# A mixer and an MLP on one core: pair 8 ahead of pair 6, tile 0's transpose copied in halves, tile 3 transposed by DMA

## The chip, the core and the metric

The kernel runs on one core of a Trainium2 chip. The core has five engines with instruction queues of their own: TensorE (PE in the profile; its weight loads are PEld), VectorE (DVE), ScalarE (ACT), GpSimd (POOL) and SyncE (SP), which here only issues DMAs. They meet through semaphores. The metric is the device time of one execution in microseconds, the median over several runs.

## What is computed

```python
B, S, D, F = 1, 2048, 512, 1792
def reference(x, w1, w2, w3, w4):
    h = _gelu(_layernorm(x, axis=-1) @ w1)
    c = D // 4          # four groups of 128 columns, shifted by +1, -1, +2, -2 rows of S
    g0 = jnp.pad(h[:, :, 0*c:1*c], ((0, 0), (1, 0), (0, 0)))[:, :S, :]
    g1 = jnp.pad(h[:, :, 1*c:2*c], ((0, 0), (0, 1), (0, 0)))[:, 1:, :]
    g2 = jnp.pad(h[:, :, 2*c:3*c], ((0, 0), (2, 0), (0, 0)))[:, :S, :]
    g3 = jnp.pad(h[:, :, 3*c:   ], ((0, 0), (0, 2), (0, 0)))[:, 2:, :]
    hs = jnp.concatenate([g0, g1, g2, g3], axis=-1) @ w2
    x1 = x + hs
    h2 = _gelu(_layernorm(x1, axis=-1) @ w3) @ w4
    return x1 + h2
```

All inputs and the output are bf16.

## The kernel before

The 2048 rows are 16 tiles of 128 rows, held with rows on the partitions. A matmul needs its operand with columns on the partitions, so each tile has to be transposed before each of the two layer norms' products: either by TensorE (four transposes of 128x128 into PSUM, then a copy to SBUF by ScalarE), or by a DMA that transposes on its way.

The first product (x normalised, times w1) is done in two ways.

- **Tiles 0 to 5, "raw"**: x itself is transposed and multiplied by w1 (`m1r`), and the norm is applied afterwards, with the column sums of w1 (`cs0`, `cs1`, `cs2`, `cs`: matmuls of ones with w1's four parts). Tiles 0 to 3 are transposed by TensorE (`tp0` to `tp3`, copied by `ev0` to `ev3`), tiles 4 and 5 by one DMA straight from DRAM (`tdx_4`). `rc` copies the raw product out of PSUM.
- **Tiles 6 to 15, in pairs**: VectorE takes statistics (`st0_`, `ag0_`), GpSimd the inverse roots (`rs0_`), VectorE normalises (`nm0_`), and then the pair is transposed, by TensorE for pairs 8 and 10 (`tp8`, `ev8`), by DMA for the others (`td0_6`). `m1p` multiplies a pair in 16 matmuls of 256 columns, `g1p` or `g1s` applies the gelu.

The second product (`m2`, with w2 and shifted windows), the second norm, `m3`/`m3h` (w3) and `m4` (w4) follow. The first half pair of `m3h` needs `td1_8`, the second `td1_10`, both DMA transposes of the normalised second layer.

Each step is an `Op` of a small program, with the resources that it reads and writes. `emit` derives the semaphore waits from these. The order on each engine is written out by hand, in `firsts`: one list of names for PE, ACT, DVE, POOL and SP. An engine runs its list strictly in order, so a step that waits holds up everything after it on its engine. On SP, where nearly all loads and all transposing DMAs are issued, the list is the DMA queue's order. PSUM has eight banks; the number given to a step (`b`) says which ones it writes, and whoever wrote or read them last must be done.

At the start the lists before are (cut):

```python
firsts["pe"] = """wu tp0 cs0 cs1 m1r01 m1r02 tp1 m1r03 cs2 m1r0 cs tp2 m1r12 m1r1 tp3 m1r2 m1r3 m1r4 m1r5 tp8 m1p6
    tp10 m1p8 m1p10 ...
firsts["act"] = """ldw10 ldw12 ldx1 table ev0 ev1 rc0 ev2 ev3 rc1 rc2 rc3 rc4 rc5 ev8 cse g1p6 ev10 g1p8 g1s10 ...
firsts["sp"] = """ldx0 ldw11 ldx6 ldw13 ldx7 ldx2 ldx8 ldx3 ldx9 tdx_4 ldx10 ldx11 ldx12 td0_6 ldx13 ...
```

`wu` is seven matmuls of ones, issued before the first data is there. `m1r01` is tile 0's product with w1's first part alone, `m1r02` with the second, and so on, so that each can start when its part has landed.

Of the kernel before, what the change touches and what calls it, by code (L numbers as in the profile page):

```python
# [5 lines left out]
P = 128  # L6
ACT_F = mybir.ActivationFunctionType
# [19 lines left out]
class Program:  # L27
# [7 lines left out]
    def add(self, eng, name, fn, reads=(), writes=(), dma=False):  # L35
        self.ops.append(Op(name, eng, fn, reads, writes, dma))
# [135 lines left out]
def bass_standalone__mixer_s_mlp__prompt_kernel(nc: bass.Bass, x, w1, w2, w3, w4, out):  # L172
# [4 lines left out]
    DC = D // P  # L177
# [5 lines left out]
    xd = x[0].rearrange("(p t) d -> p t d", t=NT)  # L183
# [4 lines left out]
    with ExitStack() as es:  # L188
        sb = lambda name, shape, dt: es.enter_context(nc.sbuf_tensor(name, shape, dt))
        x_sb = sb("x_sb", [P, NT, D], BF16)  # L190
# [3 lines left out]
        xnT = sb("xnT", [P, NT, DC, P], BF16)  # L194
# [11 lines left out]
        ident = sb("ident", [P, P], BF16)  # L206
# [3 lines left out]
        neghalf = sb("neghalf", [P, 4], F32)  # L210
# [3 lines left out]
        psb = ps[:, :].bitcast(BF16)  # L214
# [27 lines left out]
        W1 = [(("w1", c), 0) for c in range(DC)]  # L242
        W2 = [(("w2", c), 0) for c in range(DC)]
        pr = Program()
        add = pr.add

        def bank(b, n=1):
            return ps[:, 512 * b : 512 * (b + n)]

        def bres(b, n, tag):  # L250
            return [(("ps", b + i), tag) for i in range(n)]
# [19 lines left out]
        def load_x(t, n, eng="sp"):  # L271
            add(eng, f"ldx{t}", lambda e: e.dma_start(x_sb[:, t : t + n, :], xd[:, t : t + n, :]),
                writes=[(("x", i), 0) for i in range(t, t + n)], dma=True)
# [9 lines left out]
        def dst_of(layer, t):  # L283
            return (xn, t, ("xn", t), 0) if layer == 0 else (x1n, POS[t] % 8, ("x1n", POS[t] % 8), t)
# [50 lines left out]
            add(eng, f"ev{t}", f, reads=bres(b, 1, f"tp{t}"), writes=[(("xT", i), 0) for i in range(t, t + n)])  # L335


        def tdma(layer, t, n):
            dst = xnT if layer == 0 else x1nT
            src, k = dst_of(layer, t)[:2]  # L340
            p0 = t if layer == 0 else POS[t]
            add("sp", f"td{layer}_{t}",
                lambda e: e.dma_start(dst[:, p0 : p0 + n, :, :].rearrange("p t c s -> p (t c) s"),
                                      src[:, k : k + n, :].rearrange("p t d -> p (t d)"), transpose=True),
                reads=[dst_of(layer, i)[2:] for i in range(t, t + n)],
                writes=[(("xT", i) if layer == 0 else ("x1T", i), 0) for i in range(t, t + n)], dma=True)


        def tdma_x(t):
            add("sp", f"tdx_{t}",  # L350
                lambda e: e.dma_start(xnT[:, t : t + 2, :, :].rearrange("p t c s -> p (t c) s"),
                                      xd[:, t : t + 2, :].rearrange("p t d -> p (t d)"), transpose=True),
                writes=[(("xT", i), 0) for i in (t, t + 1)], dma=True)

        def tdma_h(t, n):
            add("sp", f"th_{t}",
# [17 lines left out]
        def m1r(t, b, c0=0, c1=DC):  # L374
            def f(e):
                ins = None
                for c in range(c0, c1):
                    ins = e.matmul(bank(b), xnT[:, t, c, :], w1_sb[:, c, :], start=(c == 0), stop=(c == DC - 1))  # L378
                return ins

            rd = [(("xT", t), 0)] + W1[c0:c1]
            if c0:
                rd += bres(b, 1, f"m1r{t}{c0}")
            end = f"{c1}" if c1 < DC else ""
            add("pe", f"m1r{t}{end}", f, reads=rd, writes=bres(b, 1, f"m1r{t}{end}"))

        def rc(t, b):
            add("act", f"rc{t}", lambda e: e.activation(yraw[:, t, :], bank(b), ACT_F.Copy),
                reads=bres(b, 1, f"m1r{t}"), writes=[(("yraw", t), 0)])
# [11 lines left out]
                reads=[(("zraw", t % 4), t), (("rstd", t), 0)], writes=[(("hraw", t), 0)])  # L401


        def m1p(t, b):
            def f(e):
                ins = None
                for fc in range(DC):
                    dst = ps[:, 512 * b + 256 * fc : 512 * b + 256 * (fc + 1)]
                    for c in range(DC):
                        ins = e.matmul(dst, w1_sb[:, c, P * fc : P * (fc + 1)], xnT[:, t : t + 2, c, :],  # L410
                                       start=(c == 0), stop=(c == DC - 1))
                return ins

            add("pe", f"m1p{t}", f, reads=[*W1, (("xT", t), 0), (("xT", t + 1), 0)],
                writes=bres(b, 2, f"m1p{t}"))

        def g1p(t, b):
            src = bank(b, 2).rearrange("p (j t s) -> p j t s", j=DC, t=2)
# [139 lines left out]
        load_w1(2, "act")  # L558
        load_w1(3, "sp")
        load_x(1, 1, "act")  # L560
        for t, n in ((6, 1), (7, 1), (2, 1), (8, 1), (3, 1), (9, 1), (10, 1), (11, 1), (12, 1), (13, 1), (14, 1), (15, 1), (4, 2)):
            load_x(t, n)
        for c in range(DC):
            load_w2(c)
# [7 lines left out]
            colsum(4, c)  # L572
        colsum_out(4)
        for t in range(R):
            if t < 4:
                tp(t, 1, 6 + t % 2, True)
                ev(t, 1, 6 + t % 2, "act")
            elif t == 4:
                tdma_x(t)
            cuts = [0, 1, 2, 3, 4] if t == 0 else [0, 2, 4] if t == 1 else [0, 4]  # L580
            for c0, c1 in zip(cuts, cuts[1:]):
                m1r(t, YB[t], c0, c1)
            rc(t, YB[t])
# [7 lines left out]
        for t in range(R, NT, 2):  # L591
# [2 lines left out]
                ev(t, 2, 6 + t // 2 % 2)  # L594
            else:
                tdma(0, t, 2)
        for t, b in ((6, 2), (8, 4), (10, 0), (12, 2), (14, 6)):
            m1p(t, b)
            if t == 10:
                g1s(t, b, 0)  # L600
                g1s(t, b, 1)
            else:
                g1p(t, b)
# [19 lines left out]
        for t in (8, 10):  # L623
# [7 lines left out]
            tdma(1, t, 2)  # L631

        firsts = {}
        firsts["pe"] = """wu tp0 cs0 cs1 m1r01 m1r02 tp1 m1r03 cs2 m1r0 cs tp2 m1r12 m1r1 tp3 m1r2 m1r3 m1r4 m1r5 tp8 m1p6
            tp10 m1p8 m1p10 m2_8a m2_9a m2_8 m2_9b m2_9 m2_10a m2_11a m2_12a m2_13a m1p12 m1p14 m2_10 m2_11
            m2_12b m2_13b m2_14a m2_15a m2_12 m2_13 m2_14b m2_15b m2_14 m2_15""".split()
        firsts["act"] = """ldw10 ldw12 ldx1 table ev0 ev1 rc0 ev2 ev3 rc1 rc2 rc3 rc4 rc5 ev8 cse g1p6 ev10 g1p8 g1s10 g1s11
            g1r0 g1r1 g1p12 g1p14 g2h_0_0_0 g2h_0_0_4 g1r2 g1r3 g2h_0_0_8 g2h_0_0_12 g1r4 g1r5""".split()
        firsts["dve"] = """pada padb padc padd pade padf st0_0 st0_6 st0_7 ag0_6 ag0_7
            st0_8 nm0_6 nm0_7 st0_9 ag0_8 ag0_9 st0_10 st0_11 nm0_8 nm0_9 ag0_10 ag0_11  # L640
            st0_12 nm0_10 nm0_11 st0_13 ag0_12 ag0_13 st0_14 st0_15 ag0_14 ag0_15 nm0_12 nm0_13 st0_1 ag0_0 ag0_1
            nm0_14 nm0_15 zr0 zr1 x1_8 x1_9 st1_8 st1_9 ag1_8 ag1_9 st0_2 nm1_8 nm1_9 st0_3 ag0_2 ag0_3 x1_10 x1_11 st1_10
            st1_11 ag1_10 ag1_11 x1_12 nm1_10 nm1_11 x1_13 x1_14 x1_15 zr2 zr3 st0_4 st0_5 ag0_4 ag0_5 zr4 zr5
            st1_12 st1_13 ag1_12 ag1_13""".split()
        firsts["pool"] = """ident0 ident1 neghalf stz ste rs0_6 rs0_8 rs0_10
            rs0_12 rs0_14 rs0_0 rs1_8 rs0_2 rs1_10""".split()
        firsts["sp"] = """ldx0 ldw11 ldx6 ldw13 ldx7 ldx2 ldx8 ldx3 ldx9 tdx_4 ldx10 ldx11 ldx12 td0_6 ldx13 ldx14 ldx15 ldw20 ldw21 ldw22 ldw23 td0_12 td0_14 ldw3a0 ldw3a1
            ldw3a2 ldw3a3 th_0 td1_8 ldw3b0 ldw3b1 ldw3b2 ldw3b3 ldx4 td1_10 th_2 th_4 td1_12 td1_14 ldw4""".split()

        slots = [4, 0, 2]  # L650
# [55 lines left out]
        for i, t in enumerate((0, 1, 2, 3, 4, 5, 6, 7)):  # L706
            b = (6, 7, 1)[i % 3]
# [11 lines left out]
        for q in (2, 3):  # L719
            for i in range(4):  # L720
                b = 6 + i % 2
# [40 lines left out]
```

## Time and profile before

| | |
|---|---|
| median of 3 runs | 136.61 us (136.52 to 136.8) |
| the profiled execution's own time | 136.71 us |
| its span in the profile | 134.7 us |
| PE busy | 131.6 us, 98% of the span, 729 matmuls and transposes |
| DVE, ACT, POOL busy | 58.2, 46.7, 12.5 us |
| transposes of x by TensorE (L323, from x_sb) | 16, between 3.7 and 8.3 us |
| m1r (L378) | 24 matmuls of 512 columns, between 5.0 and 11.6 us |
| m1p (L410) | 80 matmuls of 256 columns, from 12.3 us on |
| DMA queue of SP and its packets | 12.42 MB in 23984 packets, two thirds of them of 256 B |

The span counts from the first to the last instruction of the program; the rest of the device time lies around it. Matmuls overlap in the profile (their ends are modelled), so what one costs TensorE is the distance from its start to the start of the next. "L323" is a line of the kernel below a helper: all steps that the same helper records share that line, and are told apart by their place in time.

### The profile page before, as it was taken

Reading aid. Unit: us, or ns where it says so; the run is one execution under the profiler, and the core shown is the slowest. Engines: PE = TensorE matmul, PEld = TensorE weight load, DVE = VectorE, ACT = ScalarE, POOL = GpSimd, SP = SyncE. Lnnn points to the kernel's source line nnn. Section 1 sums busy time; section 2 is a strip of 40 time slices with the busy share of each in tenths; the row PEclk is TensorE's granted clock in tenths of the full one; section 3 lists DMA queues with packets and bytes.
Section 4 is the critical chain, followed back from the end, with each engine's and each line's share of the span. In section 5 each row is a group of like instructions: output and inputs, shape, how many; then the busy total and the mean of one; then the engine's idle time right before and its main releaser. Section 6 shows DMA issues by size and latency. Waiting matters only on the chain.

```text
span 134.7 us, 1809 instructions
## 1 busy us (share of the span) xinstructions
PE 131.6 (98%) x729; PEld 69.7 (52%) x729; DVE 58.2 (43%) x135; ACT 46.7 (35%) x56; POOL 12.5 (9%) x25
## 2 busy tenths in 40 slices
PE   7999999999999999999999999999999999999993
PEld 2446867668884444444444444444444444444452
DVE  0689989799967777762222000122200002322222
ACT  3387871507963035550001555200066630000000
POOL 2032422220330012220000000000000000000000
PEclk9999999999999999999999999999999999999999
DMA  3999489984465893444111000011110001111121
GB/s 110 335 230 198 145 160 246 243 276 95 78 124 101 260 298 75 81 80 78 39 61 56 5 0 0 0 39 39 39 39 5 0 0 39 39 39 39 42 76 43
DMA packets 24568, 12.96 MB, mean 96 GB/s; under 512 B 16752, under 2 KB 23920, under 8 KB 24560
## 3 DMA queue, kind: packets, MB, share of 16 engines
q1 hardware_dynamic: 23984, 12.42, 36.4%
q10 hardware_dynamic: 576, 0.43, 1.0%
q8 instruction: 6, 0.10, 0.3%
q14 instruction: 2, 0.02, 0.1%
HBM read 6.82 MB, written 2.10 MB: 66 GB/s over the span
## 4 chain that ended last, share of the span: by engine, by line
PE 98%; DVE 0%; issue 0%
PE ps L511 36%; PE ps L468 27%; PE ps L492 9%; PE ps L410 6%; PE ps L436 5%; PE ps L450 5%; PE ps L378 4%; PE ps L534 2%; PE ps L323 2%; PE ps L366 1%; DVE o_sb L523 0%
## 5 line engine op out<-in xcount | busy, mean ns | idle before, releaser
L511 PE MATMUL ps<-w_sb,h2T 128*128 128x512 bf16 (+2 forms) x238 | 48.9, 366 | 0.0
L523 DVE TENSOR_TENSOR o_sb<-ps,x_sb 128x512 bf16<-128x512 f32 (+2 forms) x17 | 11.2, 660 | 61.2 <-PE ps L511 61.2
L479 ACT ACTIVATE h2T<-ps 128x1024 bf16<-128x1024 f32 x21 | 21.5, 1024 | 46.2 <-PE ps L468 46.2
L468 PE MATMUL ps<-x1nT,w_sb 128*128 128x512 bf16 x168 | 36.8, 379 | 0.0
L511 PEld LDWEIGHTS ps<-w_sb,h2T 128*128 128x128 bf16 x238 | 22.8, 98 | 25.9
L468 PEld LDWEIGHTS ps<-x1nT,w_sb 128*128 128x128 bf16 x168 | 16.4, 98 | 19.8
L289 DVE BATCH_NORM_STATS2 st<-x_sb 128x6 f32<-128x512 bf16 x32 | 20.9, 681 | 3.9 <-DMA x_sb<-in_x_dram 3.9
L300 POOL TENSOR_TENSOR rstd<-mv,neghalf 128x2 f32<-128x2 f32 x16 | 11.6, 725 | 46.2 <-DVE mv L294 46.2
L492 PE MATMUL ps<-x1nT,w_sb 128*128 128x256 bf16 x112 | 12.4, 273 | 0.0
L460 DVE TENSOR_TENSOR x_sb<-ps,x_sb 128x512 bf16<-128x512 f32 x16 | 10.6, 686 | 2.9 <-PE ps L436 1.5
L492 PEld LDWEIGHTS ps<-x1nT,w_sb 128*128 128x128 bf16 x112 | 10.9, 98 | 1.6
L410 PE MATMUL ps<-xnT,w_sb 128*128 128x256 bf16 x80 | 9.2, 273 | 0.0
L503 ACT ACTIVATE h2T<-ps 128x1024 bf16<-128x1024 f32 (+1 forms) x8 | 7.1, 915 | 6.0 <-PE ps L492 6.0
L410 PEld LDWEIGHTS ps<-xnT,w_sb 128*128 128x128 bf16 x80 | 7.7, 98 | 1.2
L309 DVE TENSOR_SCALAR x1n<-x_sb,mv,rstd 128x512 bf16<-128x512 bf16 x16 | 5.9, 411 | 5.3 <-POOL rstd L300 5.3
L450 PE MATMUL ps<-w_sb,hTf 128*128 128x512 bf16 x32 | 7.2, 379 | 0.0
L436 PE MATMUL ps<-w_sb,hTf 128*128 128x512 bf16 x32 | 7.1, 379 | 0.0
L378 PE MATMUL ps<-w_sb,xnT 128*128 128x512 bf16 x24 | 6.4, 399 | 0.0
L420 ACT ACTIVATE hTf<-ps 128x1024 bf16<-128x1024 f32 x4 | 4.1, 1024 | 4.1 <-PE ps L410 4.1
L332 ACT ACTIVATE xnT<-ps 128x512 bf16<-128x512 bf16 (+1 forms) x6 | 4.4, 736 | 2.6 <-PE ps L323 2.6
L294 DVE BATCH_NORM_AGGREGATE mv<-st 128x2 f32<-128x9 f32 x32 | 5.0, 186 | 0.0
L436 PEld LDWEIGHTS ps<-w_sb,hTf 128*128 128x128 bf16 x32 | 3.1, 98 | 3.6
(28 smaller groups left out, 37.1 us busy)
## 6 DMA issues: line engine op xcount, KB each, us to landing
out_dram<-o_sb SPq DMA_DIRECT2D x15, 128.0 KB, 1.8
w_sb<-in_w_dram SPq DMA_DIRECT2D x1, 1792.0 KB, 8.0
x_sb<-in_x_dram SPq DMA_DIRECT2D x13, 128.0 KB, 3.2
w_sb<-in_w_dram SPq DMA_DIRECT2D x4, 256.0 KB, 4.4
w_sb<-in_w_dram SPq DMA_DIRECT2D x6, 128.0 KB, 3.1
w_sb<-in_w_dram SPq DMA_DIRECT2D x4, 192.0 KB, 3.1
w_sb<-in_w_dram ACTq DMA_DIRECT2D x2, 128.0 KB, 3.3
x_sb<-in_x_dram SPq DMA_DIRECT2D x1, 256.0 KB, 3.9
```

The lines of the kernel that those rows point to most:

```text
L289: add("dve", f"st{layer}_{t}", lambda e: e.bn_stats(st9[:, i, 0:6], src[:, t, :]), reads=[(r, 0)], writes=[(("st6", i), 0)])
L300: lambda e: e.tensor_tensor(rstd[:, i : i + n], mv[:, i : i + n, 1], neghalf[:, 0:n], ALU.pow),
L378: ins = e.matmul(bank(b), xnT[:, t, c, :], w1_sb[:, c, :], start=(c == 0), stop=(c == DC - 1))
L410: ins = e.matmul(dst, w1_sb[:, c, P * fc : P * (fc + 1)], xnT[:, t : t + 2, c, :], start=(c == 0), stop=(c == DC - 1))
L436: ins = e.matmul(bank(b), hTf[:, c0 : c0 + P], w2_sb[:, j, :], start=(j == 0), stop=(j == DC - 1))
L450: ins = e.matmul(bank(b), hTf[:, w[0] : w[0] + P], w2_sb[:, j, :], start=first and n == 0, stop=last and n == len(js) - 1)
L460: lambda e: e.tensor_tensor(x1_sb[:, t, :], bank(b), x_sb[:, t, :], ALU.add),
L468: ins = e.matmul(bank(b), w3_sb[:, c, P * fc : P * (fc + 1)], x1nT[:, 4 * q : 4 * q + 4, c, :], start=(c == 0), stop=(c == DC - 1))
L479: lambda e: e.activation(h2T[:, fc : fc + 2, q % 2, :], src, ACT_F.Gelu_apprx_tanh),
L492: ins = e.matmul(dst, w3_sb[:, c, P * (fc + i) : P * (fc + i + 1)], x1nT[:, t : t + 2, c, :], start=(c == 0), stop=(c == DC - 1))
L511: ins = e.matmul(ps[:, 512 * b : 512 * b + c1 - c0], h2T[:, fc, q % 2, P * i : P * (i + 1)], w4_sb[:, fc, c0:c1], start=(fc == 0), stop=(f ...
L523: lambda e: e.tensor_tensor(o_sb[:, k % 4, c0:c1], ps[:, 512 * b : 512 * b + c1 - c0], x1_sb[:, t, c0:c1], ALU.add),
```

## The change

- **Tile 0**: its four transposes become two steps of two, `tp0a` into bank 6 and `tp0b` into bank 7, each with its own copy (`ev0a`, `ev0b`). `m1r01` and `m1r02` need only the first half (`("xTa", 0)`).
- **Tile 3**: no longer transposed by TensorE; a DMA transposes it from DRAM (`tdx_3`), ahead of that of tiles 4 and 5 (`tdx_4`). `tp3` and `ev3` are gone. Its load into SBUF, still wanted for its statistics, moves from among the first loads to behind `td0_14`.
- **Pair 8 before pair 6**: `m1p8` runs ahead of `m1p6`, in exchanged banks; `m1p6` is cut into its first four matmuls (`m1p61`) and the other twelve, with `tp10` in between. x8 and x9 take the places of x6 and x7 in SP's list, x6 and x7 those of x8 and x3. VectorE's and GpSimd's lists take pair 8 first.
- **Order**: `cs1`, `cs2` and `cs` come later in PE's list; `m1r4` is cut in two, with `tp8` between the halves; ScalarE's list follows (`ev8` ahead of `rc4`). On SP, `td0_6` stands behind two more loads of x.

```diff
+        def tp_part(t, c0, c1, b, part, res):
+            o = 1024 * b
+            n = (c1 - c0) * P
+
+            def f(e):
+                ins = None
+                for c in range(c0, c1):
+                    k = o + (c - c0) * P
+                    ins = e.transpose(psb[:, k : k + P], x_sb[:, t, P * c : P * (c + 1)], ident[:])
+                return ins
+
+            add("pe", f"tp{t}{part}", f, reads=[(("x", t), 0), ("ident", 1)], writes=bres(b, 1, f"tp{t}{part}"))
+            add("act", f"ev{t}{part}",
+                lambda e: e.activation(xnT[:, t, c0:c1, :].rearrange("p c s -> p (c s)"), psb[:, o : o + n], ACT_F.Copy),
+                reads=bres(b, 1, f"tp{t}{part}"), writes=[(res, 0)])
...
-        def tdma_x(t):
+        def tdma_x(t, n):
             add("sp", f"tdx_{t}",
-                lambda e: e.dma_start(xnT[:, t : t + 2, :, :].rearrange("p t c s -> p (t c) s"),
-                                      xd[:, t : t + 2, :].rearrange("p t d -> p (t d)"), transpose=True),
-                writes=[(("xT", i), 0) for i in (t, t + 1)], dma=True)
+                lambda e: e.dma_start(xnT[:, t : t + n, :, :].rearrange("p t c s -> p (t c) s"),
+                                      xd[:, t : t + n, :].rearrange("p t d -> p (t d)"), transpose=True),
+                writes=[(("xT", i), 0) for i in range(t, t + n)], dma=True)
...
-            rd = [(("xT", t), 0)] + W1[c0:c1]
+            rd = [(("xTa", t) if t == 0 and c1 <= 2 else ("xT", t), 0)] + W1[c0:c1]
...
-        def m1p(t, b):
+        def m1p(t, b, f0=0, f1=DC):
...
         for t in range(R):
-            if t < 4:
+            if t == 0:
+                tp_part(0, 0, 2, 6, "a", ("xTa", 0))
+                tp_part(0, 2, 4, 7, "b", ("xT", 0))
+            elif t < 3:
                 tp(t, 1, 6 + t % 2, True)
                 ev(t, 1, 6 + t % 2, "act")
-            elif t == 4:
-                tdma_x(t)
-            cuts = [0, 1, 2, 3, 4] if t == 0 else [0, 2, 4] if t == 1 else [0, 4]
+            elif t < 5:
+                tdma_x(t, 1 if t == 3 else 2)
+            cuts = [0, 1, 2, 3, 4] if t == 0 else [0, 2, 4] if t in (1, 4) else [0, 4]
...
-        for t, b in ((6, 2), (8, 4), (10, 0), (12, 2), (14, 6)):
-            m1p(t, b)
+        for t, b in ((6, 4), (8, 2), (10, 0), (12, 2), (14, 6)):
+            if t == 6:
+                m1p(t, b, 0, 1)
+                m1p(t, b, 1, DC)
+            else:
+                m1p(t, b)
...
-        firsts["pe"] = """wu tp0 cs0 cs1 m1r01 m1r02 tp1 m1r03 cs2 m1r0 cs tp2 m1r12 m1r1 tp3 m1r2 m1r3 m1r4 m1r5 tp8 m1p6
-            tp10 m1p8 m1p10 m2_8a ...
+        firsts["pe"] = """wu tp0a tp0b cs0 m1r01 m1r02 tp1 m1r03 m1r0 cs1 tp2 m1r12 m1r1 m1r2 cs2 m1r3 m1r42 tp8 m1r4 m1r5
+            cs m1p8 m1p61 tp10 m1p6 m1p10 m2_8a ...
-        firsts["act"] = """ldw10 ldw12 ldx1 table ev0 ev1 rc0 ev2 ev3 rc1 rc2 rc3 rc4 rc5 ev8 cse g1p6 ev10 g1p8 g1s10 g1s11
+        firsts["act"] = """ldw10 ldw12 ldx1 table ev0a ev0b ev1 ev2 rc0 rc1 rc2 rc3 ev8 rc4 rc5 cse g1p8 ev10 g1p6 g1s10 g1s11
-        firsts["dve"] = """pada padb padc padd pade padf st0_0 st0_6 st0_7 ag0_6 ag0_7
-            st0_8 nm0_6 nm0_7 st0_9 ag0_8 ag0_9 st0_10 st0_11 nm0_8 nm0_9 ag0_10 ag0_11
+        firsts["dve"] = """pada padb padc padd pade padf st0_0 st0_8 st0_9 ag0_8 ag0_9
+            st0_6 st0_7 ag0_6 ag0_7 nm0_8 nm0_9 nm0_6 nm0_7 st0_10 st0_11 ag0_10 ag0_11
-        firsts["pool"] = """ident0 ident1 neghalf stz ste rs0_6 rs0_8 rs0_10
+        firsts["pool"] = """ident0 ident1 neghalf stz ste rs0_8 rs0_6 rs0_10
-        firsts["sp"] = """ldx0 ldw11 ldx6 ldw13 ldx7 ldx2 ldx8 ldx3 ldx9 tdx_4 ldx10 ldx11 ldx12 td0_6 ldx13 ldx14 ldx15 ldw20 ldw21 ldw22 ldw23 td0_12 td0_14 ldw3a0 ldw3a1
+        firsts["sp"] = """ldx0 ldw11 ldx8 ldw13 ldx9 ldx2 ldx6 ldx7 tdx_3 tdx_4 ldx10 ldx11 ldx12 ldx13 ldx14 td0_6 ldx15 ldw20 ldw21 ldw22 ldw23 td0_12 td0_14 ldx3 ldw3a0 ldw3a1
```

## The prediction

> **What bounds the kernel now.** First the page: its busy table, its chain, its fetches.
>
> ```profile
> PE 131.6 (98%) x729; PEld 69.7 (52%) x729; DVE 58.2 (43%) x135; ACT 46.7 (35%) x56; POOL 12.5 (9%) x25
> ...
> PE 98%; DVE 0%; issue 0%
> ...
> q8 instruction: 6, 0.10, 0.3%
> ```
>
> TensorE is the chain, so a microsecond is won or lost only where its own stream gets shorter or waits. Second, the timeline of PE, cut to the start, to see whether it ever waits. Columns: start, length, count; lengths overlap, so I read the distances between starts.
>
> ```profile
> 0.78 3.14 PE L534 MATMUL ps<-const-bfloat16-1.0 128*128 128x512 bf16 x7 [0.78 <-PEq L747]
> 3.74 0.61 PE L323 MATMUL ps<-ident,x_sb 128*128 128x128 bf16 x4
> 4.14 1.06 PE L366 MATMUL ps<-w_sb,const-bfloat16-1.0 128*128 128x512 bf16 x2
> 5.04 1.03 PE L378 MATMUL ps<-w_sb,xnT 128*128 128x512 bf16 x2
> ...
> 8.14 0.39 PE L323 MATMUL ps<-ident,x_sb 128*128 128x128 bf16 x4
> 8.37 3.62 PE L378 MATMUL ps<-w_sb,xnT 128*128 128x512 bf16 x16
> 11.82 0.61 PE L323 MATMUL ps<-ident,xn 128*128 128x128 bf16 x8
> 12.27 1.91 PE L410 MATMUL ps<-xnT,w_sb 128*128 128x256 bf16 x16
> 14.01 0.61 PE L323 MATMUL ps<-ident,xn 128*128 128x128 bf16 x8
> ```
>
> Until 6.1 us a 512-column matmul takes 427 ns from start to start, after that 216; 128 columns take 107, then 56; 256 columns 109. Taking these off every distance leaves 2.6 us of slow start, 0.04 at the first m1r (5.04) and 0.06 near 34.5. Nothing else: TensorE waits almost nowhere. So the change can win the work it takes out and little more, and it loses wherever its new order makes TensorE wait.
>
> Third, SP's queue, since every load and every DMA transpose is issued there one after another.
>
> ```profile
> 2.61 2.36 SPq L272 DMA_DIRECT2D x_sb<-in_x_dram  x5
> 5.01 1.39 SPq L351 DMA_TRANSPOSE xnT<-in_x_dram  x1
> 6.45 1.52 SPq L272 DMA_DIRECT2D x_sb<-in_x_dram  x3
> 8.60 1.26 SPq L343 DMA_TRANSPOSE xnT<-xn  x1
> ```
>
> A load holds SP for 0.47, a two-tile transpose for 1.24 to 1.39. In the DMA view, cut to one issue each, the transposes land 4.2 us (tdx_4, tiles 4 and 5 from DRAM) and 3.4 (td0_6, tiles 6 and 7) after their start: at 9.23 and 12.03.
>
> **Part by part.** *Tile 3's transpose leaves TensorE.* Four transposes, 8.14 to 8.37: 0.22 us gone from a stream without gaps. Its ScalarE copy ev3 goes too (0.60, in idle time; nothing gained).
>
> *Tile 0 in halves.* A copy of 1024 columns takes 1.02, of 512 0.60, so 256 take about 0.39. tp0a ends at 4.14 by its last record, ev0a runs 4.18 to 4.57, and m1r01 starts at 4.62 where cs0 ends at 4.57: 0.03 to 0.05 of wait, as the 0.04 that it has now behind two column sums. Zero net. cs1, cs2 and cs move later in the stream and cost the same there or half: but what they give up before 6.1 other matmuls take up, so again nothing.
>
> *Inputs of the early steps.* The five loads in front keep their places: x2, fourth x load of SP, landed at 6.4 (start 3.08 plus 3.3); tp2 now wants it at 6.6. w1's last part lands at 5.7, m1r0 starts at 6.2. x1 lands at 5.3, tp1 at 5.45. ev2 ends at 7.66 where m1r2 wants it at 7.7: exactly covered; if it slips, the cost is its slip. Each of these covers is 0 to 0.5 us thick.
>
> *Tiles 3, 4 and 5 by DMA.* SP reaches tdx_3 at 4.50 (the place where x9's load stood). No row shows a one-tile transpose: its issue lies between a load's 0.43 and the two-tile 1.39; I take 0.9, half-way, as half the tile count would have it. tdx_4 then starts at 5.45 instead of 5.01. m1r3 is due at 8.8 (8.37 less 0.22 and less the two column sums now behind it, 0.43, gives m1r2 at 7.7; four matmuls and cs2 follow), m1r42 at 9.65. tdx_3 lands by 8.7 if it takes the two-tile 4.2, about 8 with half the packets: covered. tdx_4: moved with its start it lands at 9.67; counted by the queue, x9's 128 packets of 1 KB (0.4 us) in front of it are replaced by 512 of 256 B (the two-tile transpose's packets run from 6.5 to 8.5, so a half of it is 0.5 to 0.9), and it lands at 9.3 to 9.7. From the best start-to-landing of such a transpose (3.1) to the worst in the trace (5.2, the first of hraw) it is 8.6 to 10.65: a wait of 0 to 1.0. I take 9.5 and a wait of 0; it is the thinnest cover of the change, 0.15 us.
>
> *Pair 8 first.* x8, x9 sit where x6, x7 sat; VectorE's chain is the same with one more statistics ahead of the norms (0.6), so norm 9 ends at 9.1; tp8 is due at 10.1. ev8 ends at 11.75, m1p8 is due at 12.04. Pair 6's transpose: norms 6 and 7 follow by 0.85, to 9.97; SP has by then passed five loads behind tdx_4 (6.84 + 2.5 = 9.4), so td0_6 is issued at 10.0 instead of 8.6 and lands at 13.4 (3.4 as now). It is wanted by m1p61 at 13.8 instead of 12.27. Cost 0, and 0.4 at 4.2 from start to landing. cse must free bank 4 before m1p61: it ends at 13.3. ev10 lies between g1p8 and g1p6 with the same 2.2 us from the end of the first pair to m1p10 as before (16 and 8 instructions between, now the second pair's 12, tp10's 8 and the 4 ahead of it): no change. The cut of m1r4 and of m1p6 adds no matmul.
>
> *x3's load moved to the end.* Queued behind it on SP: w3's eight parts, th_0, td1_8, ldx4, td1_10; each issues 0.47 later unless it waited anyway. x3's statistics are at 23.6 (lands about 21.5). w3's first half landed at 25.1, wanted at 28.1: nothing. But the queue is full of w3 from 20 to 31 us, so 128 KB more in it can push td1_10, whose landing makes the wait of 0.06 near 34.5:
>
> ```profile
> 34.37 0.44 PE L492 MATMUL ps<-x1nT,w_sb 128*128 128x256 bf16 x2
> ...
> 34.54 0.38 PE L492 MATMUL ps<-x1nT,w_sb 128*128 128x256 bf16 x2
> ```
>
> These two neighbours start 170 ns apart instead of 109. td1_10 takes 4.8 from start to landing (29.61 to 34.4), although its packets end at 32.4. The DMA view of 31.9 to 33.4 has one instruction fetch, and the packet list puts it at 32.39, for 0.93 us, ahead of the last semaphore packet of one engine; the other fifteen had landed by 32.86.
>
> ```profile
> q1 hardware_dynamic: 175, 0.04, 13.1%
> q8 instruction: 1, 0.02, 3.9%
> ```
>
> The fetches of this queue come about every 256 instructions of TensorE (191, 446, 685, 927 done at four of them). Eight instructions fewer put it 8 further into the work: 4 pairs of 109 ns later, less the 0.22 gained: 32.6. td1_10's packets move by -0.2 (with the norms) to +0.4 (128 KB of full queue), against 0.2 that the fetch moves. I take it that they get out in front: the 0.06 goes. If not, see below.
>
> Sum: -0.22 (tp3) - 0.06 (34.5) + 0.02 (m1r01, ev2) = -0.26. Against the profiled execution's own 136.71 (span 134.7, 2.0 around it) that is 136.45; the median of the runs, 136.61, lies 0.10 below the profiled one, so 136.35. About 0.2%, 0.27 us, is what a measurement of this kernel can tell from no change: the forecast lies on that edge.
>
> **Rivals.** *The DMA transposes land late (slower).* One mechanism: three tiles of m1r hang on transposes in the fullest stretch of the queue (the windows view has the DMA engines busy all of 2.7 to 9.6), tdx_4 behind tdx_3. It decides from a landing past 9.65; past 9.9 it eats the gain, past 10.2 it is slower beyond doubt. At 5.2 from start to landing: a wait of 1.0, 137.35; at the 10.2 in the middle, 136.9. For it: an unseen one-tile transpose and a cover of 0.15. Against it: less ordinary traffic in front than now. The Trainium skill speaks against the step too (VectorE: DVE Perf Modes, the sections on the three transpose paths and the rules for authors): a 128x128 transpose belongs on TensorE if PSUM will do, 390 ns against 1309 by DMA. The trace agrees on the order of the two (0.22 of TensorE's time per tile against 3.1 to 5.2 to a landing), but the second is not TensorE's time while it is covered.
>
> *td1_10 stays behind the fetch, with more left.* If it slips by more than 0.2 it lands at the fetch's end, 33.5, plus the 1.1 seen from there to the landing: 34.65, where TensorE is due at 34.2: 0.4 of wait in place of 0.06, 136.8, and more where more packets are left behind the fetch.
>
> *td0_6 late:* with 4.2 instead of 3.4, 14.2 against 13.8: 0.4, 136.75; with 5.2, 1.4.
>
> *The slow start gets longer.* If a wait in 2.7 to 6.1 kept the half rate for as long again as it lasts now (5.3 us, half of it lost), +2.6: 139. The granted clock in the windows view is 1.00 there, so only the 427 ns show it. For it: tp0a's shorter cover. Against it: 0.04 of wait is all that I find, as before. By the Trainium skill (TensorE: Matmul & The Clock Gate, Part 1) the array opens after a busy window of 3.4 us that runs freely; an estimate from it is +1.7. No run here shows a missed window.
>
> *The change does nothing:* the transposes are out of the stream, which I cannot see failing.
>
> **How the numbers follow.** All in time: 0.60, at 136.35 (136.41 if the 0.06 stays); 0.36 of it at a gain over 0.27, which needs a hundredth more than the sum, and 0.24 within. DMA transposes late: 0.20 (0.17 slower, 0.03 within). Behind the fetch: 0.12 (half slower, since 136.8 is still within). td0_6: 0.05 (0.03 slower, 0.02 within). Slow start: 0.03, slower. So faster 0.36, same 0.35, slower 0.29. The range begins at 136.15 (0.30 at most to win, and 0.15 of spread between runs) and goes up to 136.95, which takes in the middle of the late landing and the two cases near 136.8, and leaves out the worst landing and the slow start.
>
> **What would show it.** In the changed profile m1r3's first start near 8.8, m1r4's near 9.65 with the next 216 ns on; a wait of PEld on the xnT of a DMA there is the late landing. m1p8 at 12.05, m1p6's first at 13.8; L492 in even steps of 109 near 34.3; the fetch at 32.6. One-tile issue of 0.9 at 4.5. Steps of 427 ns past 6.1, or any gap over 0.1 before 18 us, make the forecast wrong.

## The result and the profile after

| | before | after |
|---|---|---|
| median | 136.69 us (14 runs) | 137.19 us (14 runs) |
| ratio of the times | | 1.0037, interval 1.0022 to 1.0052 |
| span, mean | 134.63 us (35 runs beside `again_before`) | 134.82 us (12 of its runs) |
| device time less span, mean | 2.10 us (the same 35) | 2.37 us (the same 12) |
| the profiled execution: time, span | 136.71, 134.7 us | 137.06, 134.4 us |

The change makes the kernel slower by 0.5 us; 136.35 was forecast, and 137.19 lies above the range. Two of the 14 runs of after took 138.9 and 139.4 us, with spans 2 us longer (none of 150 runs of before took over 137.3), one run each of `after_tail4`, `after_tp3` and `before_wu4` 139.2 to 139.6, and one of `after_sums_early` 790; these are left out of the means, and since none was profiled, a longer slow start, one of the prediction's rivals, is not ruled out for them.

The two halves of the loss are seen in the last rows but one: 0.2 us inside the span and nearly 0.3 us outside it. The profiled execution of after is one whose span came out short (134.4) and whose end came out long (137.06 less 134.4 is 2.65), so it must not be read as the mean.

The page of after, at the lines that were shown of before (busy table, fetches, chain):

```profile
PE 130.2 (97%) x715; PEld 69.2 (51%) x725; DVE 58.1 (43%) x135; ACT 46.1 (34%) x56; POOL 12.6 (9%) x25
...
q8 instruction: 5, 0.08, 0.2%
q14 instruction: 2, 0.02, 0.0%
...
PE 94%; DMA 3%; ACTq 1%; issue 1%; DVE 0%
```

PE's share of the chain fell from 98% to 94%, and a DMA stands in it with 3%: the chain now runs through the load of x1, from its issue at 1.67 to its landing at 5.67, and TensorE waits for that landing. (Some matmul records are missing, hence x715 beside 725 weight loads.) One fetch of TensorE's instructions (q8) is gone from the span; it comes back below. The timeline of PE, cut to the same stretch as before's (start, length, count):

```profile
3.71 0.62 PE L346 MATMUL ps<-ident,x_sb 128*128 128x128 bf16 x4
4.14 0.41 PE L383 MATMUL ps<-w_sb,const-bfloat16-1.0 128*128 128x512 bf16 x1
4.61 0.60 PE L395 MATMUL ps<-w_sb,xnT 128*128 128x512 bf16 x2
5.71 0.40 PE L323 MATMUL ps<-ident,x_sb 128*128 128x128 bf16 x4 [0.50 <-DMA x_sb<-in_x_dram]
5.95 0.59 PE L395 MATMUL ps<-w_sb,xnT 128*128 128x512 bf16 x2
6.38 0.38 PE L383 MATMUL ps<-w_sb,const-bfloat16-1.0 128*128 128x512 bf16 x1
6.59 0.39 PE L323 MATMUL ps<-ident,x_sb 128*128 128x128 bf16 x4
6.82 1.89 PE L395 MATMUL ps<-w_sb,xnT 128*128 128x512 bf16 x8
8.54 0.38 PE L383 MATMUL ps<-w_sb,const-bfloat16-1.0 128*128 128x512 bf16 x1
8.76 1.49 PE L395 MATMUL ps<-w_sb,xnT 128*128 128x512 bf16 x6
10.09 0.61 PE L323 MATMUL ps<-ident,xn 128*128 128x128 bf16 x8
...
12.04 2.35 PE L427 MATMUL ps<-xnT,w_sb 128*128 128x256 bf16 x20
```

`tp1` (5.71) waits 0.50 for x1, which landed at 5.67. `tp2` (6.59) starts 0.06 behind x2's landing (6.53). The first is a gap over 0.1, which the prediction had named as a sign of being wrong. In before `tp2` started at 7.06, 0.66 behind the landing: TensorE ran at half rate until 6.1 there, and had two more column sums to do. Here full rate begins at 4.6, and the two sums, 0.43 us of TensorE, stand behind `tp2` (8.54 and 11.83). From there on every step is where the prediction put it: `m1r3` 8.76, `tp8` 10.09, `m1p8` 12.04. That is luck: the waits for x1 and x2 happen to take as long as the longer half rate would have, and in the next profile of after, below, the same steps come 0.7 to 0.8 later. SP's queue (start, length, count):

```profile
2.61 1.86 SPq L272 DMA_DIRECT2D x_sb<-in_x_dram  x4
4.51 2.65 SPq L368 DMA_TRANSPOSE xnT<-in_x_dram  x2
7.21 2.48 SPq L272 DMA_DIRECT2D x_sb<-in_x_dram  x5
10.17 1.25 SPq L360 DMA_TRANSPOSE xnT<-xn  x1
```

Two transposes take 2.65 together, the one-tile one 1.31 of it. The neighbours that stood 170 ns apart near 34.5 in before are in even steps of 109 here, and the fetch is at 32.55.

Last, the DMA view of after from 135.3 to 139 us, behind its last instruction (134.41), by queue:

```profile
q8 instruction: 1, 0.02, 1.9%
q14 instruction: 1, 0.01, 0.8%
```

Both are instruction fetches, at 136.15 (16 KB) and 136.35 (8 KB), when no instruction is left to run. In before the packet list has TensorE's sixth fetch at 130.27 and nothing behind the end.

### The profile page after: what moved, and what is told of

Read it like the earlier page. It is cut to its first block, busy times and chain, and to the rows that moved or that the text cites. A ratio compares the mean times of both kernels' runs of the same rounds, so it can differ in the third digit from the quotient of the medians.

```text
span 134.4 us, 1794 instructions
## 1 busy us (share of the span) xinstructions
PE 130.2 (97%) x715; PEld 69.2 (51%) x725; DVE 58.1 (43%) x135; ACT 46.1 (34%) x56; POOL 12.6 (9%) x25
## 4 chain that ended last, share of the span: by engine, by line
PE 94%; DMA 3%; ACTq 1%; issue 1%; DVE 0%
PE ps L531 36%; PE ps L488 27%; PE ps L512 9%; PE ps L427 7%; PE ps L456 5%; PE ps L470 5%; PE ps L395 4%; DMA x_sb<-in_x_dram 3%; PE ps L323 1%; ACTq L562 1%; PE ps L383 0%; DVE o_sb L543 0%
## 5 line engine op out<-in xcount | busy, mean ns | idle before, releaser
L531 PE MATMUL ps<-w_sb,h2T 128*128 128x512 bf16 (+2 forms) x232 | 48.1, 366 | 0.3
L456 PEld LDWEIGHTS ps<-w_sb,hTf 128*128 128x128 bf16 x32 | 3.1, 98 | 3.6
L470 PEld LDWEIGHTS ps<-w_sb,hTf 128*128 128x128 bf16 x32 | 3.1, 98 | 3.3 <-ACT hTf L445 0.2
```

Source lines behind the costliest of these rows:

```text
L456: ins = e.matmul(bank(b), hTf[:, c0 : c0 + P], w2_sb[:, j, :], start=(j == 0), stop=(j == DC - 1))
L470: ins = e.matmul(bank(b), hTf[:, w[0] : w[0] + P], w2_sb[:, j, :], start=first and n == 0, stop=last and n == len(js) - 1)
L531: ins = e.matmul(ps[:, 512 * b : 512 * b + c1 - c0], h2T[:, fc, q % 2, P * i : P * (i + 1)], w4_sb[:, fc, c0:c1], start=(fc == 0), stop=(f ...
```

## The experiments

"Span" is the mean over the runs of a kernel, "outside" the mean of device time less span. Before has 134.58 to 134.67 and 2.1 in all comparisons. A mean of twelve spans is good to 0.05 to 0.1 us; `after_tail4_sp`, `after_loads_first` and `after_tp3` have five or six runs, and the means of the last two are good to 0.3 and 0.15. Each kernel ran beside before on its chip.

**Both kernels again.**

> The kernel before once more, for its spans, its second profile and the spread of its early waits. Theory of the loads (the changed order reaches the loads of x1 and x2 too early, because the column sums that used to lie there come later): its wait ahead of tp1 is small in every profile, 0 to 0.3 us, and its spans vary by less than 0.5 us. Theory of the end (the difference lies outside the span, after the last instruction): the time outside the span is about 2.0 us in all its runs, against 2.1 to 2.75 of the changed kernel.

> The changed kernel once more. Theory of the loads: its spans scatter with the moment at which the clock opens and the loads land, median about 134.8 us, and the profile shows 0.3 to 0.7 us of wait ahead of tp1 or tp2. Theory of the end: spans at or below those of before, and 0.2 to 0.6 us more outside the span. Theory of the late DMA transposes: a wait of over 0.2 us at m1r3 or m1r42.

Measured: 136.75, ratio 1.0002 (0.9988 to 1.0016), span 134.67, outside 2.07; and 137.23, 1.0034 (1.001 to 1.0058), span 134.92, outside 2.33 (4 of 12 runs between 2.67 and 2.87). The loss and its two halves are there again. The profiles show how far an execution of the same kernel can move. PE of the kernel before, run again, around `tp2`:

```profile
6.77 0.38 PE L366 MATMUL ps<-w_sb,const-bfloat16-1.0 128*128 128x512 bf16 x1
7.18 0.40 PE L323 MATMUL ps<-ident,x_sb 128*128 128x128 bf16 x4
```

and PE of the kernel after, run again:

```profile
6.42 0.40 PE L323 MATMUL ps<-ident,x_sb 128*128 128x128 bf16 x4 [0.92 <-DMA x_sb<-in_x_dram]
...
7.09 0.38 PE L383 MATMUL ps<-w_sb,const-bfloat16-1.0 128*128 128x512 bf16 x1
7.35 0.40 PE L323 MATMUL ps<-ident,x_sb 128*128 128x128 bf16 x4
```

x2 landed at 7.13 in the first and at 7.30 in the second, against 6.40 and 6.53 in the first two profiles: 0.7 later, with the same program. In both, `tp2` starts 0.05 behind the landing. So x2's landing is a gate that moves by 0.7 us, and the profile that the forecast was worked out from happened to have it open early. There it did not hold up before at all, because TensorE, at half rate until 6.1, came to `tp2` later still; in the profile of `before_halves`, with x2 at 6.41 too but full rate from 4.6, `tp2` starts at 6.49. Behind `tp2` these four profiles do not move: TensorE's end less `tp2`'s start is 125.3 in both profiles of before and 125.5 in both of after, 0.22 less for `tp3` and 0.43 more for two column sums. An estimate from the mean spans (less these, less the 2.33 from TensorE's end to the span's) has `tp2` start at 7.0 to 7.1 in both kernels: on the mean, what after does not compute ahead of `tp2` is spent waiting.

**The column sums, alone.**

```diff
before_sums_late (from before)
- wu tp0 cs0 cs1 m1r01 m1r02 tp1 m1r03 cs2 m1r0 cs tp2 m1r12 m1r1 tp3 m1r2 m1r3 m1r4 m1r5 tp8 m1p6
+ wu tp0 cs0 m1r01 m1r02 tp1 m1r03 m1r0 cs1 tp2 m1r12 m1r1 tp3 m1r2 cs2 m1r3 m1r4 m1r5 cs tp8 m1p6
after_sums_early (from after)
- wu tp0a tp0b cs0 m1r01 m1r02 tp1 m1r03 m1r0 cs1 tp2 m1r12 m1r1 m1r2 cs2 m1r3 m1r42 tp8 m1r4 m1r5 cs m1p8
+ wu tp0a tp0b cs0 cs1 m1r01 m1r02 tp1 m1r03 cs2 m1r0 cs tp2 m1r12 m1r1 m1r2 m1r3 m1r42 tp8 m1r4 m1r5 m1p8
```

> The kernel before with the column sums late, as the changed one has them (cs1 ahead of tp2, cs2 ahead of m1r3, cs ahead of tp8); all else as before. Theory of the loads: it waits for x1 and x2, and is 0.2 to 0.5 us slower than before. Theory of the end and of the late DMA transposes: no change, within 0.1.

> The changed kernel with the four column sums back at the places that they had before (cs1 behind cs0, cs2 ahead of m1r0, cs behind it). Theory of the loads: the sums fill the time that TensorE otherwise waits, so the spans fall by 0.2 to 0.4 us against the changed kernel, to 134.4 to 134.6, and none is 2 us longer. Theory of the end: span and time outside it stay as in the changed kernel, within 0.1. Theory of the late DMA transposes: no gain either.

Measured: sums late in before 136.97, 1.0014 (1.0003 to 1.0026), span 134.86, so 0.23 lost inside the span and nothing outside (2.09). Sums early in after 137.12, 1.0036 (1.001 to 1.0062), span 134.90: nothing won. The first is as the gate would have it; the second is not. In its profile x1 landed at 5.94 and x2 at 7.22, so that its sums, too, waited. From there TensorE needs 125.0, 0.43 less than in after, as it should; by the same estimate as above `tp2` then starts near 7.5 on the mean, 0.4 later than in after. Why, with the same loads in the same order, is not known.

**The end of the run.**

```diff
after_tail4 (from after; behind everything else)
+        warmup("tail", 4, 1)        # four matmuls of ones, 8 instructions
after_tail4_sp (from after_tail4; x13 and x14 in one DMA, one issue of SP fewer)
-  (13, 1), (14, 1),      ldx13 ldx14 td0_6
+  (13, 2),               ldx13 td0_6
```

> The changed kernel with four matmuls of ones added at the very end of TensorE's program, behind the last matmul, while the last output is still on its way (8 instructions; the change took 6 off the program's count with its waits, 1480 to 1474). Theory of the end: the sixth 16 KB fetch comes back near 130 us, and the time outside the span falls from a mean of 2.35 (a part of the runs at 2.6 to 2.9) to the 2.1 of before; the span stays at 134.8 to 134.9. If the end has to do with the work of the change and not with the count, it stays at 2.35.

> The changed kernel with the four matmuls at the end and with x13 and x14 in one load, so that SP issues as many DMAs as in the kernel before. Theory: the 8 KB fetch of the other queue, which all profiles of the changed order show near 136.7 and none of before, is SP's and goes with its one more transpose; the time outside the span falls from 2.20 to 2.08, as before. If it belongs to another engine, it stays at 2.20. The span stays at 134.85.

Measured: 137.15, 1.0026 (1.0013 to 1.0038), span 134.84, outside 2.20 with 2.30 as its highest; then 137.29, 1.0038 (1.0024 to 1.0053), span 135.18, outside 2.10. With four useless matmuls more, TensorE's sixth fetch is back at 130.83, inside the run, and the long ends (2.6 and more, in a third of after's runs) are gone: 0.17 of the mean. With one issue of SP fewer the 8 KB fetch behind the end is gone as well: another 0.10. Together these are the loss outside the span. Its cause is no work but a count: after has 1474 instructions on TensorE where before has 1480, and 61 DMA issues on SP where before has 60. The profiles show how the fetches set the end. In all seven with a fetch behind the last instruction, the time outside is 0.24 us less than what lies between the span's end and the end of the later fetch. Where that is TensorE's (`after`, `after_addr`, `after_loads_first_addr`), it ends 2.88, 3.18 and 3.06 behind the span, and the time outside is 2.65, 2.94 and 2.82; where it is SP's, it ends 2.45 to 2.52 behind, and the time outside is 2.21 to 2.29. In the thirteen profiles without one the time outside is 2.05 to 2.18. The span of the second kernel, 0.34 longer, was not expected; see the rows.

**Fewer matmuls at the start.** `warmup("wu", 7, 5)` to `warmup("wu", 4, 5)` in before, which takes six instructions out of before as the change does.

> The kernel before with 4 warm-up matmuls instead of 7: 6 instructions fewer, 1474 as in the changed kernel, the removed ones in time in which TensorE waits for x0 anyway. Theory of the end: the fetch near 130 us is gone and the time outside the span rises from 2.1 to about 2.35. Otherwise it stays at 2.1. The span shows the clock rule besides: if a hole of 1.3 us ahead of 3.7 us keeps the slow start going, it grows by up to 1.7 us in a part of the runs; if not, it stays within 0.2 of 134.65.

Measured: 138.23, 1.0087 (1.0056 to 1.0118), span 135.70, outside 2.10 as the median and 2.89 in one run of 8. The fetch near 130 is gone from the profile, but the long end came only once: a partial hit. The span shows something else, in the timeline of PE:

```profile
6.98 0.63 PE L378 MATMUL ps<-w_sb,xnT 128*128 128x512 bf16 x1
7.40 0.63 PE L366 MATMUL ps<-w_sb,const-bfloat16-1.0 128*128 128x512 bf16 x1
7.83 0.62 PE L323 MATMUL ps<-ident,x_sb 128*128 128x128 bf16 x4
```

Starts 0.43 apart up to 8.3, where before changes to 0.216 at 6.1. That is the missed start of full speed that the prediction had as a rival; it costs half of 2.2 us, and the span is 1.07 longer.

**Tile 0 in halves, alone** (`tp0` cut into `tp0a` and `tp0b` in before, nothing else).

> The kernel before with tile 0's transposes and copies in halves and nothing else. My prediction: zero, since cs0 and cs1 cover the copy either way; span within 0.1 of 134.63, time outside 2.08 (two semaphore steps more, no instruction of TensorE less). Theory of the gate: the same zero, since x2 decides.

Measured: 136.62, 1.0002 (0.9988 to 1.0015), span 134.59. No effect, as predicted.

**The gate's own loads first on SP.**

```diff
before_loads_first
- ldx0 ldw11 ldx6 ldw13 ldx7 ldx2 ldx8 ldx3
+ ldx0 ldw11 ldw13 ldx2 ldx6 ldx7 ldx8 ldx3
after_loads_first
- ldx0 ldw11 ldx8 ldw13 ldx9 ldx2 ldx6 ldx7
+ ldx0 ldw11 ldw13 ldx2 ldx8 ldx9 ldx6 ldx7
```

> The kernel before with w1's last part and x2 ahead of x6 and x7. Theory of the gate: tp2 starts up to 0.4 us earlier in runs whose clock opens early, but x6 and x7 land 0.6 later, norm 7 ends at 9.2 instead of 8.6 and td0_6 lands at 12.6, 0.3 behind m1p6: the span stays within 0.2 of 134.63. If the loads do not gate tp2, it only loses: 134.8 to 135.

> The changed kernel with w1's last part and x2 ahead of x8 and x9 in SP's queue; nothing else. Theory of the gate (tp2 starts when x2 has landed, whatever lies before it, and what the change moved behind tp2, two column sums of 0.43 less tp3's 0.22, is added to the time): x2 lands near 6, tp2 starts when TensorE gets there, 6.3 to 6.6 instead of a mean of 7.07, and the span falls by 0.2 to 0.4 us, to 134.5 to 134.65, where td0_6 (13.7 to 14.0) stops it. Theory of the late DMA transposes or of the order alone: no change from 134.85. If x8 and x9, now later, hold up norm 9, tp8 waits and the span rises.

Measured: 137.35, 1.0051 (1.0033 to 1.0069), span 135.35; and 137.90, 1.0092 (1.006 to 1.0123), span 135.82. Both slower, both expectations missed. In before x2 came earlier (5.74), but now the statistics of the first pair are late, and `tp8` waits 0.17 for them and `m1p6` 0.04 for `td0_6`. That is 0.2 in a profile with a span of 134.78; the rest of the 0.7 that the mean lost was not traced. In after it did not even open the gate: x1 landed at 6.83 and x2 at 7.01, though x2 had been moved ahead of two other loads. The loads as a whole were slow.

**Which rows the early loads read.** In after the two loads among w1's parts read tiles 8 and 9 where before reads 6 and 7: the same size, another place in DRAM. These kernels exchange only the place (tile 6's buffer takes tile 8's rows, and so on).

```diff
-            add(eng, f"ldx{t}", lambda e: e.dma_start(x_sb[:, t : t + n, :], xd[:, t : t + n, :]),
+            s = {6: 8, 7: 9, 8: 6, 9: 7}.get(t, t)
+            add(eng, f"ldx{t}", lambda e: e.dma_start(x_sb[:, t : t + n, :], xd[:, s : s + n, :]),
```

> The kernel before, but the loads of tiles 6, 7 take the DRAM rows of tiles 8, 9 and the other way round: same instructions, sizes and order, other addresses (the output has these tiles computed from the other's rows). Theory of the addresses (x8's rows land later in this place than x6's, and push x1, w1's last part and x2, which share the queue): x1 and x2 land 0.2 to 0.4 us later after w11, and the span grows by 0.2, to 134.85. Theory of the order alone: no change, within 0.1.

> The changed kernel with the same exchange of addresses, so that its early loads read the rows that the kernel before reads there. Theory of the addresses: the span falls by 0.2 to 0.4 us, to 134.4 to 134.6; the time outside it stays at 2.35. Theory of the order alone (TensorE reaches the loads too early whatever they read): span unchanged at 134.8 to 134.9.

> The changed kernel with w1's last part and x2 ahead of x8 and x9, and with the DRAM rows of tiles 6, 7 and 8, 9 exchanged in the loads (the output has these tiles from the other's rows). Without the exchange x1 landed at 6.8 and x2 at 7.0, and 436 KB came between 3.5 and 5.5 us, against 631 in the kernel before with the same order. Theory of the addresses: with x6's and x7's rows in these places 600 to 690 KB come in that stretch, x1 lands at 5.2 to 5.6, x2 below 6.4, and the span falls from 135.8 to 134.6. Theory of the one-tile DMA transpose (it slows the loads around it): no change, x1 at 6.2 to 6.8, span 135.5 to 135.9.

> The changed kernel with four matmuls at its end, x13 and x14 in one load, and the same exchange of rows. Theory of the addresses: 600 to 690 KB between 3.5 and 5.5 us instead of 480, the span falls from 135.18 to 134.6 or 134.7, time outside it 2.08 to 2.10, 136.7 in all, as before. Theory of the one-tile transpose: span 135.1 to 135.2.

| kernel | span, rows of 8 and 9 early | span, rows of 6 and 7 early |
|---|---|---|
| before | 134.75 (`before_addr`) | 134.63 |
| after | 134.87 | 134.68 (`after_addr`) |
| after_tail4_sp | 135.18 | 134.68 |
| after_loads_first | 135.82 | 135.14 |

(134.87 is the mean of after's two.) All four go the same way: 0.12, 0.19, 0.50 and 0.68. The first two are hardly larger than their uncertainty of 0.1 each; in the last two the partners ran on different chips, on which before differs by 0.03. Of the four expectations of the theory of the addresses only that of `after_tail4_sp_addr` was met; `after_loads_first_addr` came half-way. The medians: `before_addr` 136.76, 1.0009 (0.9992 to 1.0027), alone no difference; `after_addr` 136.97, 1.0034 (1.0013 to 1.0056), with its long ends still there (outside 2.42); `after_tail4_sp_addr` 136.72, 1.0007 (0.9997 to 1.0016); `after_loads_first_addr` 137.16, 1.0045 (1.0023 to 1.0067).

**Tile 3 back on TensorE.** In after, `tp3` and `ev3` again (`tp3` ahead of `m1r2`), no `tdx_3`, x3's load in its place.

> The changed kernel with tile 3 transposed by TensorE again (tp3 behind m1r1, x3's load where tdx_3 stood). Theory of the addresses: the loads are as slow as in the changed kernel (480 to 655 KB between 3.5 and 5.5 us), and the span rises by tp3's 0.22 to 135.0 to 135.1, less where td0_6, now issued nearly 1 us earlier at most, had held it. Theory of the one-tile transpose: the loads are as fast as before, tp2 starts 0.2 to 0.4 earlier, and the span is at or below 134.8.

Measured: 137.68, 1.0071 (1.0052 to 1.0091), span 135.46, outside 2.08 (no fetch behind the end): slower than either expectation. Tile 3's DMA transpose is not what makes after slow; without it the span is 0.6 longer. `tp3` is 0.2 of that: in the profile TensorE's end less `tp2`'s start is 125.7, against 125.5 in after. The rest would lie ahead of `tp2`, near 7.5 on the mean by the estimate used above; the one profile (`tp2` at 7.04, span 135.03) does not show it.

**The change with its side effects taken out.** Three more kernels. `pairs_back` is `after_tail4_sp` with the pairs' roles exchanged: TensorE transposes pair 6 first, `td0_8` does pair 8, and x6 and x7 have the early places. `pairs_back_sums_early` also has the column sums where before has them. `tp10_ahead` also has `tp10` ahead of `m1p81`.

```diff
pairs_back (from after_tail4_sp)
- m1r42 tp8 m1r4 m1r5 cs m1p8 m1p61 tp10 m1p6      ldx0 ldw11 ldx8 ldw13 ldx9 ldx2 ldx6 ldx7
+ m1r42 tp6 m1r4 m1r5 cs m1p6 m1p81 tp10 m1p8      ldx0 ldw11 ldx6 ldw13 ldx7 ldx2 ldx8 ldx9
pairs_back_sums_early
- cs0 m1r01 m1r02 tp1 m1r03 m1r0 cs1 tp2 m1r12 m1r1 m1r2 cs2 m1r3 m1r42 tp6 m1r4 m1r5 cs m1p6
+ cs0 cs1 m1r01 m1r02 tp1 m1r03 cs2 m1r0 cs tp2 m1r12 m1r1 m1r2 m1r3 m1r42 tp6 m1r4 m1r5 m1p6
tp10_ahead
- m1p6 m1p81 tp10 m1p8 m1p10
+ m1p6 tp10 m1p81 m1p8 m1p10
```

> The kernel after with the roles of the two pairs exchanged, so that the early places in the queue are x6's and x7's again and TensorE transposes pair 6 first (td0_8 now does pair 8), and with both end-of-run instruction fetches kept away (four matmuls of ones behind the last one, x13 and x14 in one load); the result is complete. If the rows that are read early matter: early loads as in the exchanged kernels, span 134.6 to 134.75 and 2.09 around it, 136.7 to 136.8, ratio 1.000 to 1.001. If the exchanged rows only mattered because data were mixed up, or the three differences were chance: span 135.0 to 135.2 as with the tail and the joined load, ratio 1.003 to 1.004.

> The same with the column sums where before had them (cs0 and cs1 ahead of m1r01, cs2 ahead of m1r0, cs ahead of tp2). If what they fill ahead of tp2 is free waiting time for x1 and x2, the span falls by the 0.2 that moving them late cost in the kernel before: 134.4 to 134.5, 136.5 to 136.6, ratio 0.998 to 0.999, which would be the fastest so far. If td0_8's landing is the next to arrive late (m1p81 comes two column sums earlier there), it stays within 0.1 of the other run.

> pairs_back_sums_early with tp10 moved ahead of m1p81 in TensorE's list. In the profile of that kernel m1p81 waited for td0_8's landing (13.91): its first start is 0.49 behind the one before it, 0.38 more than the 0.109 of a matmul, and norm 11, which tp10 needs, had ended at 13.55. If the late landing of the DMA pair is what is left of the loss, tp10's 0.44 fills the wait: 0.25 to 0.35 gone, span 134.2 to 134.3, 136.3 to 136.4, ratio 0.997 to 0.998, faster than before. If the landing only moves along with the early loads, or norm 11 is late in most runs, it stays within 0.1 of 134.54.

Measured:

| | median | ratio | span | outside |
|---|---|---|---|---|
| after_tail4_sp | 137.29 | 1.0038 (1.0024 to 1.0053) | 135.18 | 2.10 |
| pairs_back | 136.75 | 1.0003 (0.999 to 1.0016) | 134.72 | 2.11 |
| pairs_back_sums_early | 136.66 | 0.9994 (0.9981 to 1.0006) | 134.54 | 2.12 |
| tp10_ahead | 136.52 | 0.9989 (0.9977 to 1.0) | 134.44 | 2.08 |

The first three ran on the same chip. Exchanging the pairs back takes 0.46 from the span, as much as exchanging the rows in DRAM did (0.50). The windows view shows the early traffic, from 3.5 to 5.5 us (last column: GB/s), of `after_tail4_sp`:

```profile
3.50:5.50 2.00, 1.55 (x8) 0.59 (x7) 0.69 (x1) 0.81 (x3) 0.00 (x0) 1.00 0.90 246
```

and of `pairs_back`:

```profile
3.50:5.50 2.00, 2.00 (x9) 0.69 (x9) 1.06 (x2) 0.81 (x3) 0.00 (x0) 1.00 1.08 368
```

Loads of the same sizes, issued at the same times within 0.02 us, move at 246 GB/s in one and 368 in the other; x2 lands at 7.58 and at 6.40. Over all profiles taken, rows of 6 and 7 early have 306 to 368 in this window (and 260 once, in `after_loads_first_addr`), rows of 8 and 9 early 223 to 336, with means of 336 over 12 and 282 over 8 profiles: the two overlap, so that one profile alone does not tell them apart.

The rest of what the gate gives is lost behind it. With the early loads in time, `tp2` starts at 6.47 in `pairs_back`, `m1r42` is due at 9.50, and `tdx_4`, which transposes tiles 4 and 5, lands only at 9.67. PE and PEld in that kernel:

```profile
8.64 1.68 PE L395 MATMUL ps<-w_sb,xnT 128*128 128x512 bf16 x6
...
9.71 0.11 PEld L395 LDWEIGHTS ps<-w_sb,xnT 128*128 128x128 bf16 x2 [0.54 <-DMA xnT<-in_x_dram]
```

The weight load, which runs ahead, waits 0.54, the matmuls 0.21 (`m1r42` starts at 9.72). Later `m1p81` waits 0.23 for `td0_8`.

With the column sums early, the span falls by another 0.18: what `before_sums_late` lost. Here the loads were in time and the place of the sums counted. The timeline of PE in that kernel shows what came next:

```profile
11.83 1.91 PE L427 MATMUL ps<-xnT,w_sb 128*128 128x256 bf16 x16
13.95 0.61 PE L427 MATMUL ps<-xnT,w_sb 128*128 128x256 bf16 x4 [0.21 <-DMA xnT<-xn]
14.40 0.61 PE L323 MATMUL ps<-ident,xn 128*128 128x128 bf16 x8
```

`m1p81` waits for `td0_8`, which landed at 13.91: 0.38 more than the 0.109 from one start to the next. `tp10_ahead` puts `tp10` into that wait:

```profile
11.95 1.91 PE L427 MATMUL ps<-xnT,w_sb 128*128 128x256 bf16 x16
13.69 0.61 PE L323 MATMUL ps<-ident,xn 128*128 128x128 bf16 x8
14.14 2.03 PE L427 MATMUL ps<-xnT,w_sb 128*128 128x256 bf16 x17
```

No wait is left there. But its span is only 0.13 below before's in its own comparison (134.58), and the kernel without the step was 0.13 below as well (134.67): 134.2 to 134.3 was expected and not reached, and a gain of the step is not shown. It has the lowest ratio of the case, and its interval just touches no change.

## Why the prediction was wrong, point by point

- **Tile 3's -0.22, the wait of 0.06 near 34.5, tile 0 at zero.** Right. 125.3 less 0.22 plus the two column sums' 0.43 is the 125.5 found, the wait is gone with the fetch at 32.55 (32.6 was forecast), and `before_halves` shows the zero.
- **"cs1, cs2 and cs move later in the stream and cost the same there or half: ... so again nothing".** This is the step that failed first. It counted the column sums as work that TensorE has to do somewhere, and missed that ahead of `tp2` they stood in time in which TensorE would wait for x2 in many executions. Moved behind the gate they cost their 0.43 in full and save only a part of it in front. Measured: 0.23 lost in before, 0.18 in the kernels with the pairs back. `after_sums_early` did not show it.
- **"Inputs of the early steps. The five loads in front keep their places".** The places, yes, but not the rows. And each landing was taken from one profile to 0.1 us, with covers of "0 to 0.5", where the landing of x2 moves by 0.7 between executions. A cover thinner than that is a cost in a part of the runs; it was counted as zero. The half rate, too, was taken to last until 6.1 as in that profile, though the prediction itself quotes that its window runs freely. Measured for the rows: 0.19 in after itself, with an uncertainty of 0.1, and 0.5 with the tail and the joined load.
- **"2.0 around it".** The forecast took the time outside the span as fixed. It grew by 0.23 to 0.27, by two instruction fetches behind the end. The prediction had counted the instructions to place the fetch near 32.4 (eight fewer; it is six, since TensorE got two waits more) and did not ask where the last one went.
- **Added up:** -0.28 for `tp3` and the wait, 0.23 for the sums, 0.19 for the rows, 0.27 outside: 0.41 of the 0.46 that the means show (0.19 and 0.27). With 0.1 of uncertainty on the sums and on the rows, that it comes so close is partly luck.
- **The rival of late DMA transposes** did not happen in after's two profiles (waits of at most 0.02, with `tp2` at 6.59 and 7.35), but its cover was as thin as feared. `tdx_3`'s issue was 1.31, not the 0.9 estimated, as long as a two-tile one, and `tdx_4` landed at 9.46 to 10.02 in the profiles of the kernels with `tdx_3`, where 9.5 was taken and 9.65 was the limit. Where `tp2` started at 6.42 and 6.47, TensorE waited: 0.20 for `tdx_4` and 0.18 for `tdx_3` in `after_tail4_sp_addr`, 0.21 for `tdx_4` in `pairs_back`; in `pairs_back_sums_early` 0.09 for `tdx_3`. The Trainium skill's rule against the step (VectorE: DVE Perf Modes, the rules for authors: a 128x128 transpose on TensorE if PSUM will do) is not borne out here: `after_tp3`, which follows it for tile 3, needs 0.2 us more of TensorE behind `tp2` and is not faster.
- **The rival of td1_10 behind the fetch** did not happen in after. **td0_6 late** happened in part: it landed at 13.6 to 14.3 where 13.4 was forecast (at 14.65 and 15.0 in the two kernels with the gate's loads first, whose TensorE is later too), with no wait in the two profiles of after, up to 0.18 in its variants, and 0.23 and 0.38 with the pairs back.
- **The slow start** did not happen in any profile with seven matmuls at the start. `before_wu4` shows its price. The Trainium skill has the window run freely (TensorE: Matmul & The Clock Gate, Part 1), with an estimate of 1.7 from it in the prediction; the trace agrees that the opening moves (between 4.0 and 6.1 in the profiles with seven matmuls, 8.3 with four), and the one missed opening cost 1.07, less than that estimate.

What stays open: why the rows of tiles 8 and 9 are read more slowly ahead of the rest than those of 6 and 7; why in before the difference is only 0.12; why joining x13 and x14 went with 0.34 more in the span (`after_tail4_sp` has six runs, on another chip than `after_tail4`); why the early sums won nothing in after; and what `after_tp3` lost beyond `tp3`'s 0.22.

## What to carry to other kernels

Work that stands ahead of a wait costs nothing as long as the wait would last anyway, whatever it costs by the row: before moving it, look in several profiles for the landing that ends that wait, and treat a cover thinner than its spread as a cost. A load that keeps its place in the queue but reads other rows can be another load in time. When a few tenths of a microsecond decide, look at what runs behind the last instruction, too: the count of instructions alone moved the end by 0.3 us.

## What the runs showed of the hardware that was not expected

- TensorE's instructions come in 16 KB fetches, one for about every 256. With six instructions fewer the sixth is at 136.15 instead of 130.27, behind the last instruction, and a third of the runs end at 2.6 to 2.9 us outside the span instead of 2.1. In all seven profiles with a fetch behind the last instruction the time outside follows the end of the later fetch, at 0.24 us less. The Trainium skill (Runtime: NRT & Kernel Launch, Instruction fetch mechanics) has blocks of 256 instructions too, and calls the cost mostly hidden; at the end of this kernel it was not.
- A transposing DMA from DRAM holds SP for 1.30 or 1.31 us with one tile and for 1.29 to 1.55 with two, over all profiles.
- Early loads of the same sizes, issued at the same times, moved at 246 and at 368 GB/s in two kernels that differ in which rows of x come first; over all profiles the means are 282 and 336.
